# Moving the tensor that takes all loads to a multiple of 4096 bytes in a partition

## The chip, the cores and the metric

The kernel runs on one core of a Trainium2 chip. The metric is the device time of one execution in microseconds (us), the median of several runs.

## The reference

One decoding step: attention of a single query over a long cache of keys and values, a small gated feed-forward block beside it, and a gate that mixes the two.

```python
# x [1,1,512]; k_cache, v_cache [1,32,65536,128]; wq [512,4096]; wo [4096,512]; all bf16
q = (x @ wq) split into 32 heads of 128
scores = einsum("bhqd,bhkd->bhqk", q, k_cache) * 128 ** -0.5
o = einsum("bhqk,bhkd->bhqd", softmax(scores), v_cache)
a = o.reshape(1, 1, 4096) @ wo
b = (silu(x @ w_gate) * (x @ w_up)) @ w_down        # 512 -> 1792 -> 512
g = sigmoid((x * gate_w).sum(-1))
out = g * a + (1 - g) * b
```

The two caches are 537 MB each, and every byte of them is used once.

## The kernel before

A head's keys (16 MiB) come in two loads of 8 MiB, the values likewise. Partition p receives 256 consecutive cache rows of 128 numbers, so a load is 128 partitions with one contiguous stretch of 64 KB each, in HBM and in SBUF alike. This text calls such a stretch a row. Some loads at the beginning and the end have shorter rows: the weights (32 KB, three times 14 KB, 31 KB), the first keys in two halves (32 KB), and the last half of the last head's values in pieces of 128, 64, 32, 16, 12 and 4 cache rows (`tail`), so that little work is left when the last piece has landed.

All of these go into one SBUF tensor, `mem`, 184 KB of a partition (`MEM * KB` numbers of 2 bytes). `at(kb, n)` names n numbers at offset kb in KB. Keys lie at offsets 32 and 0 (`KA`, `KZ`), values at 120 and 96 (`VA`, `VZ`), each 64 KB long, so that the stretches overlap and a load waits for a part of the work on what lay there. All places are whole KB.

The loads are issued by SyncE (SP) in a fixed order: K and V of the heads in turn (`load`, L222 to L249), each behind a wait on how far VectorE (`ktdone`) or TensorE (`pvdone`) has come with the data that it overwrites.

For each head, VectorE transposes the keys out of `mem` into the double buffer `kt` (L322 for the first head, L415 and L422 for the others), 16 operations of 128x2048 words. TensorE multiplies them by the query in `qcur` (L472), the scores stand in one bank, ScalarE turns them into exponentials in `pa` (L288), VectorE moves these between partitions into `pb` (L331), and TensorE multiplies `pb` by the values in `mem` (L525). The value work of a head runs beside the key work of the next.

The tensors lie in a partition in the order in which `sb` allocates them. In the program before, `mem` begins at byte 16512, behind 16 KB that are reserved and four constants of 32 bytes each; `kt` follows at 204928, `qd` at 221312, and the small ones behind it.

Of the kernel before, what the change touches and what calls it, by code (L numbers as in the profile page):

```python
# [5 lines left out]
P = 128  # L6
KB = 512
PR = 32
# [4 lines left out]
BF16 = mybir.dt.bfloat16  # L13
F32 = mybir.dt.float32
U32 = mybir.dt.uint32
# [6 lines left out]
def bass_gated_mix__mha_block_cached__swiglu_ffn__decode_kernel(  # L22
# [27 lines left out]
    MEM = 184  # L50
# [12 lines left out]
    WOJ, WO31 = V0, V0 + 1  # L63

    with ExitStack() as ctx:
        def sb(name, shape, dt):
            return ctx.enter_context(nc.sbuf_tensor(name, shape, dt))

        def psum(name, shape, dt):
            return ctx.enter_context(nc.psum_tensor(name, shape, dt))  # L70
# [10 lines left out]
        psW = psum("psW", [P, 512], F32)  # L81
        psZ = psum("psZ", [P, 512], F32)

        mem = sb("mem", [P, MEM * KB], BF16)
        kt = sb("kt", [P, 2, 2 * PR * 32], U32)
        qd = sb("qd", [P, H, 4, 4], BF16)
        qcur = sb("qcur", [P, 4, 4], BF16)
        pa = sb("pa", [P, 512], BF16)
        pb = sb("pb", [P, 512], BF16)
        orow = sb("orow", [P, 512], F32)  # L90
        ident = sb("ident", [P, 128], F32)
        ones = sb("ones", [P, 2], BF16)
        onesf = sb("onesf", [P, 128], F32)
        hot = sb("hot", [P, 2, 2], F32)
# [536 lines left out]
```

## Time and profile before

| | |
|---|---|
| median of 3 runs | 2518.53 us (2518.48 to 2519.13) |
| span of the profiled execution | 2517.0 us |
| time of the profiled execution beside its span | not listed by itself; the median is 1.5 us above the span |
| instructions | 51694 |
| read from HBM | 1087.77 MB |
| busiest compute engine | PE, 68% of the span |
| granted TensorE clock, mean | 0.721 |

The profile is one execution as the hardware profiler recorded it; the span goes from the first to the last instruction. PE is TensorE's matmuls, PEld its weight loads, DVE is VectorE, ACT ScalarE, SP SyncE. A line such as `L525 PE MATMUL psO<-mem,pb ... x3968 | 1042.3, 429 | 34.5 <-DMA ...` gives a source line, the engine, the operation, what it writes and reads, how often, its busy time in us, the mean of one in ns, and the engine's idle time before it with what ended it. The chain is the work that ended last, followed back from the end; its rows in order of time are start, duration and what it was. In the DMA part, a packet is one row of a load (or the small write that reports a load's completion), and a share is the packets' time as a share of what 16 DMA engines have.

### The profile page before, as it was taken

The page shows a single profiled execution, that of the slowest core. Times are in us where ns is not written, and L with a number is a line of the kernel's source. Part 1 is how long each engine was busy: PE and PEld are TensorE (multiplying, and loading weights), DVE is VectorE, ACT ScalarE, POOL GpSimd, SP SyncE. Part 2 cuts the span into 40 slices and gives each one's busy share as a digit, 9 for nine tenths or more (in the row PEclk, how much of TensorE's full clock was granted, in tenths as well). Part 3 has the DMA queues.
Part 4 walks back from the last instruction along what each step waited for, and adds up shares of the span by engine and source line. Part 5 has one row for each costly group of instructions (what it writes and reads, how often), then busy time and mean ns, then how long its engine had stood idle before and what let it go on. Part 6 is the DMA issues. An engine that isn't in the chain of part 4 may idle for free.

```text
span 2517.0 us, 51694 instructions
## 1 busy us (share of the span) xinstructions
PE 1710.9 (68%) x21624; PEld 979.2 (39%) x21624; DVE 1411.7 (56%) x1683; ACT 64.6 (3%) x195; POOL 0.2 (0%) x4
## 2 busy tenths in 40 slices
PE   4667756667667677676776766766767767667677
PEld 3334433333433334333443333343334433334334
DVE  4764565554655645646456555465564564645653
ACT  0000000000000000000000000000000000000000
POOL 0000000000000000000000000000000000000000
PEclk8577767677677676776776767767767767677677
DMA  9999999999999999999999999999999999999999
GB/s 419 435 433 433 433 433 433 433 434 433 434 433 433 433 433 433 433 433 433 433 433 433 433 433 434 435 433 434 434 433 433 434 434 433 433 433 433 434 433 395
DMA packets 20471, 1087.93 MB, mean 432 GB/s; under 512 B 2283, under 2 KB 2669, under 8 KB 2925
## 3 DMA queue, kind: packets, MB, share of 16 engines
q1 hardware_dynamic: 20452, 1087.78, 99.9%
q8 instruction: 9, 0.15, 0.0%
q14 instruction: 2, 0.01, 0.0%
q10 hardware_dynamic: 8, 0.00, 0.0%
HBM read 1087.77 MB, written 0.00 MB: 432 GB/s over the span
## 4 chain that ended last, share of the span: by engine, by line
DMA 71%; PE 27%; DVE 1%; issue 1%; SPq 0%; ACT 0%; DVEq 0%
DMA mem<-in_A_v_cache_dram 68%; PE psO L525 27%; DMA mem<-in_A_k_cache_dram 2%; DVE kt L322 1%; DMA mem<-in_A_wq_dram 0%; DVE kt L415 0%; SPq L224 0%; PE psM L456 0%; DVE pb L331 0%; PE psS L472 0%; SPq L258 0%; PE psZ L600 0%; DVE sm L336 0%; PE psW L561 0%; PE psM L547 0%
## 5 line engine op out<-in xcount | busy, mean ns | idle before, releaser
L472 PE MATMUL psS<-qcur,kt 128*128 128x4 bf16 x16384 | 573.0, 169 | 728.7 <-DVE kt L415 413.2
L525 PE MATMUL psO<-mem,pb 128*4 128x512 bf16 x3968 | 1042.3, 429 | 34.5 <-DMA mem<-in_A_v_cache_dram 34.1
L472 PEld LDWEIGHTS psS<-qcur,kt 128*128 128x128 bf16 x16384 | 534.0, 105 | 792.1 <-issue 789.7
L422 DVE STREAM_TRANSPOSE kt<-mem 128x2048 uint32<-128x2048 uint32 x248 | 547.6, 2275 | 405.9 <-DMA mem<-in_A_k_cache_dram 405.9
L415 DVE STREAM_TRANSPOSE kt<-mem 128x2048 uint32<-128x2048 uint32 x248 | 551.3, 2280 | 239.3 <-DMA mem<-in_A_k_cache_dram 238.3
L525 PEld LDWEIGHTS psO<-mem,pb 128*4 128x4 bf16 x3968 | 359.8, 93 | 660.4 <-issue 241.3
L331 DVE COPY pb<-pa 32x64 bf16<-32x64 bf16 x1024 | 233.5, 228 | 15.1 <-ACT pa L288 1.5
L338 DVE TENSOR_REDUCE sc<-psM 1x1 f32<-1x128 f32 x32 | 8.9, 279 | 334.9 <-PE psM L547 334.9
L336 DVE TENSOR_REDUCE sm<-psS 128x1 f32<-128x512 f32 x32 | 22.1, 692 | 42.2 <-PE psS L472 42.2
L322 DVE STREAM_TRANSPOSE kt<-mem 128x2048 uint32<-128x2048 uint32 x16 | 35.4, 2277 | 16.9 <-DMA mem<-in_A_k_cache_dram 16.9
L286 ACT ACTIVATE sm<-psM 128x1 f32<-128x1 f32 x32 | 5.5, 171 | 1223.4 <-PE psM L549 1223.4
L282 ACT ACTIVATE oTn<-psT,gcol 128x1 f32 (+1 forms) x31 | 8.2, 264 | 1036.8 <-PE psT L499 1036.8
L499 PE MATMUL psT<-ident,orow 4*128 4x1 f32 x256 | 33.5, 248 | 0.5 <-ACT orow L280 0.5
L499 PEld LDWEIGHTS psT<-ident,orow 4*128 4x128 f32 x256 | 30.8, 186 | 1.2 <-ACT orow L280 0.6
L280 ACT ACTIVATE orow<-psO,sm 4x512 f32<-4x512 f32 x31 | 21.0, 678 | 130.3 <-PE psO L525 126.0
L288 ACT ACTIVATE pa<-psS,sm 128x512 bf16<-128x512 f32 x32 | 22.0, 687 | 1.0
L549 PE MATMUL psM<-sc,onesf 1*128 1x1 f32 x64 | 12.3, 259 | 11.9 <-DVE sc L338 11.9
L561 PE MATMUL psW<-pb,mem 128*128 128x1 bf16 x512 | 14.6, 165 | 6.5 <-DMA mem<-in_A_v_cache_dram 6.0
L549 PEld LDWEIGHTS psM<-sc,onesf 1*128 1x128 f32 x64 | 9.6, 186 | 21.5 <-DVE sc L338 21.5
L561 PEld LDWEIGHTS psW<-pb,mem 128*128 128x128 bf16 x512 | 14.1, 102 | 7.6 <-issue 5.5
L553 PEld LDWEIGHTS psM<-sm,onesf 128*128 128x128 f32 x64 | 9.7, 191 | 14.7 <-issue 13.5
L553 PE MATMUL psM<-sm,onesf 128*128 128x1 f32 x64 | 12.4, 264 | 1.1 <-ACT pa L288 1.1
(72 smaller groups left out, 93.1 us busy)
## 6 DMA issues: line engine op xcount, KB each, us to landing
mem<-in_A_v_cache_dram SPq DMA_DIRECT2D x3, 4096.0 KB, 29.4
mem<-in_A_k_cache_dram SPq DMA_DIRECT2D x2, 4096.0 KB, 38.9
mem<-in_A_wq_dram SPq DMA_DIRECT2D x1, 4096.0 KB, 12.3
mem<-in_A_wo_dram SPq DMA_DIRECT2D x1, 3968.0 KB, 36.6
mem<-in_A_v_cache_dram SPq DMA_DIRECT2D x1, 2048.0 KB, 32.9
mem<-in_B_w_gate_dram SPq DMA_DIRECT2D x1, 1792.0 KB, 16.1
mem<-in_B_w_up_dram SPq DMA_DIRECT2D x1, 1792.0 KB, 21.4
mem<-in_B_w_down_dram SPq DMA_DIRECT2D x1, 1792.0 KB, 25.2
```

Of the source, the lines that this page charges most:

```text
L288: nc.scalar.activation(pa[:], psS[:], ACT.Exp, bias=nbias, scale=SCALE, accum_out=rsum).then_inc(expdone, 1)
L322: nc.vector.transpose(kt[:, i % 2, :].rearrange("p (j r t) -> p r j t", j=2, t=32), src.rearrange("p (r j t) -> p r j t", j=2, t=32)).then ...
L331: last = nc.vector.tensor_copy(dst, sr)
L336: nc.vector.reduce_max(mxs, psS[:], AX_X).then_inc(s_mx, 1)
L415: nc.vector.transpose(kt[:, c % 2, :].rearrange("p (j r t) -> p r j t", j=2, t=32), src.rearrange("p (r j t) -> p r j t", j=2, t=32)).then ...
L422: nc.vector.transpose(kt[:, c % 2, :].rearrange("p (j r t) -> p r j t", j=2, t=32), src.rearrange("p (r j t) -> p r j t", j=2, t=32)).then ...
L472: last = nc.tensor.matmul(psS[:, o:o + 4] if j is None else psS[:, ds(j * (2 * PR) + o, 4)], ktb[b][:, je // 2, r, :, je % 2], qcur[:, je, ...
L499: last = nc.tensor.matmul(psT[:, 0:1], orow[0:4, i * Dh:(i + 1) * Dh], ident[0:4, i:i + 1], start=(i == 0), stop=(i == 3))
L525: last = nc.tensor.matmul(psO[0:4, :], pb[:, k_col[256 * z + r]:k_col[256 * z + r] + 4], vt[:, r * Dh:(r + 4) * Dh], start=(z == 0 and par ...
L549: nc.tensor.matmul(amx, onesf[0:1, :], gm, start=True, stop=True).then_inc(s_ar, 1)
L553: nc.tensor.matmul(Lt, onesf[:], rsum, start=True, stop=True).then_inc(s_L, 1)
L561: last = nc.tensor.matmul(psW[:, 0:1], vt[:, r * Dh:(r + 1) * Dh], pb[:, col:col + 1], start=(r0 + r == 0), stop=(r0 + r == R - 1))
```

## The change

Four small buffers, 3584 bytes together, are allocated ahead of `mem`, and `mem` asks for an alignment of 4096 bytes, which places it at byte 20480; `kt` and the other buffers follow it as before, in nearly the same order. No instruction, wait, load or size changes.

```diff
-        def sb(name, shape, dt):
-            return ctx.enter_context(nc.sbuf_tensor(name, shape, dt))
+        def sb(name, shape, dt, align=32):
+            return ctx.enter_context(nc.sbuf_tensor(name, shape, dt, align_bytes=align))
...
-        mem = sb("mem", [P, MEM * KB], BF16)
-        kt = sb("kt", [P, 2, 2 * PR * 32], U32)
         qd = sb("qd", [P, H, 4, 4], BF16)
-        qcur = sb("qcur", [P, 4, 4], BF16)
         pa = sb("pa", [P, 512], BF16)
         pb = sb("pb", [P, 512], BF16)
+        ident = sb("ident", [P, 128], F32)
+        mem = sb("mem", [P, MEM * KB], BF16, 4096)
+        kt = sb("kt", [P, 2, 2 * PR * 32], U32)
+        qcur = sb("qcur", [P, 4, 4], BF16)
         orow = sb("orow", [P, 512], F32)
-        ident = sb("ident", [P, 128], F32)
```

## The prediction

> **What bounds the kernel now.** I read the page of the profile first: its busy shares, its slices, its DMA part and its chain.
>
> ```profile
> span 2517.0 us, 51694 instructions
> PE 1710.9 (68%) x21624; PEld 979.2 (39%) x21624; DVE 1411.7 (56%) x1683; ACT 64.6 (3%) x195; POOL 0.2 (0%) x4
> DMA  9999999999999999999999999999999999999999
> GB/s 419 435 433 433 433 433 433 433 434 433 434 433 433 433 433 433 433 433 433 433 433 433 433 433 434 435 433 434 434 433 433 434 434 433 433 433 433 434 433 395
> DMA packets 20471, 1087.93 MB, mean 432 GB/s; under 512 B 2283, under 2 KB 2669, under 8 KB 2925
> ...
> q1 hardware_dynamic: 20452, 1087.78, 99.9%
> ...
> DMA 71%; PE 27%; DVE 1%; issue 1%; SPq 0%; ACT 0%; DVEq 0%
> ```
>
> No compute engine is busy for more than 68% of the span. The 16 DMA engines are busy for 99.9% of it on one queue, and the rate is flat at 433 to 435 GB/s in every slice between the first and the last. The kernel is a stream of loads. The chain gives 27% to PE, but the DMA share says that the engines kept moving data meanwhile, so I look at how the chain repeats, in order of time.
>
> ```profile
> 154.46 27.79 DMA mem<-in_A_v_cache_dram
> 182.25 0.04 issue
> 182.29 10.12 PE psO L525 x40
> ...
> 2359.93 28.29 DMA mem<-in_A_v_cache_dram
> ...
> 2477.68 36.14 DMA mem<-in_A_v_cache_dram
> 2513.82 0.05 issue
> 2513.86 0.65 PE psW L561 x16
> 2514.51 0.12 issue
> 2514.63 0.74 PE psZ L600 x7
> 2515.37 0.02 issue
> 2515.39 0.26 ACT fin L300
> ```
>
> One value load is issued at 154.46 us; the same point of the pattern, 19 repetitions later, is 2359.93 us. A repetition holds six loads (three of K, three of V), so a load takes 2205.47 / 114 = 19.346 us of the queue. A load is 8 MiB, 128 rows of 64 KB, eight rows for each of the 16 engines: 19.346 / 8 = 2418.3 ns per row, 433.6 GB/s, which is the rate of the slices. A value load lands 27.8 us after its issue and needs 19.3 us itself, so it lay queued some 8 us behind the load before it. That lead is the cover under which PE's 10.12 us of values and everything else on the compute engines hides. After the last landing at 2513.82 us only 1.8 us of work follows up to 2515.65 us. So what can move the end is the time of a row in the DMA engines, and little else.
>
> **What a row costs.** The DMA view of a window 10 ns long, chosen so that just one packet starts in it, gives that packet's duration: the share times 16 engines times 10 ns. Its bytes are the mean GB/s times 10 ns. Here are loads of 65536, 16384, 4096 and 1024 B rows, a packet of 4 B (a load's completion count), and a 256 B store of the output into HBM (queue 10).
>
> ```profile
> DMA packets 1, 0.07 MB, mean 6554 GB/s; under 512 B 0, under 2 KB 0, under 8 KB 0
> q1 hardware_dynamic: 1, 0.07, 1511.2%
> ...
> DMA packets 1, 0.02 MB, mean 1638 GB/s; under 512 B 0, under 2 KB 0, under 8 KB 0
> q1 hardware_dynamic: 1, 0.02, 381.9%
> ...
> DMA packets 1, 0.00 MB, mean 410 GB/s; under 512 B 0, under 2 KB 0, under 8 KB 1
> q1 hardware_dynamic: 1, 0.00, 99.4%
> ...
> DMA packets 1, 0.00 MB, mean 102 GB/s; under 512 B 0, under 2 KB 1, under 8 KB 1
> q1 hardware_dynamic: 1, 0.00, 28.8%
> ...
> DMA packets 1, 0.00 MB, mean 0 GB/s; under 512 B 1, under 2 KB 1, under 8 KB 1
> q1 hardware_dynamic: 1, 0.00, 5.6%
> ...
> DMA packets 1, 0.00 MB, mean 26 GB/s; under 512 B 1, under 2 KB 1, under 8 KB 1
> q10 hardware_dynamic: 1, 0.00, 9.4%
> ```
>
> That is 2417.9, 611.0, 159.0, 46.1, 9.0 and 15.0 ns. From 4096 to 65536 B the time rises by 2258.9 ns for 61440 B: 27.20 B per ns and engine. Over bytes divided by 27.20, the four loads stand at +8.5, +8.6, +8.4 and +8.4 ns. So a row has a price of its own of about 8.5 ns, whatever its length, and the rest is a straight rate; nothing is paid for each 4 KB or each 256 B inside a row, or the longer rows would show it. The spacing of 2418.3 ns says that rows follow one another without overlap or gap: 2418.3 - 2409.4 = 8.9 ns per row is on the path, completion counts included.
>
> This bounds the change from below. The profile's page has 20471 packets, 2283 of them under 512 B; the other 18188, over 16 engines, make 1136 rows each. If the whole surplus of 8.9 ns went, that would be 1136 x 8.9 ns = 10.1 us. Nothing about an address can give more unless the 27.20 B per ns itself rises, and the rows show one rate from 4 KB to 64 KB.
>
> **The change, part by part.** *The big tensor's address.* In the program before, `mem` begins at byte 16512 of a partition, which is 64 x 256 + 128: every load row begins and ends 128 B past a multiple of 256. Afterwards it begins at 20480, and as all places in `mem` are whole KB, every row begins and ends at a multiple of 256, those of the 8 MiB loads at multiples of 4096 too. No load is added, removed or reordered, and the addresses in HBM stay. All 1136 rows per engine are on the path.
>
> What of the 8.5 ns belongs to the odd start? Below, nothing (the row price is the turnover from one descriptor to the next). Above, all 8.9 ns. The nearest row between is the store: its destination rows in HBM are 256 B apart and start even, and it stands at 15.0 - 256 / 27.20 = +5.6 ns, 2.8 ns less than a load (though its source, `fin`, begins 96 B past a multiple of 256, so it isn't fully even either). The mechanism that I take for likeliest lies between these ends: a row that begins in the middle of a 256 B line is worked from the line's beginning, so the 128 B in front pass through the engine for nothing, 128 / 27.20 = 4.7 ns per row. The end of the row, a half line, costs its bytes alone. That makes 1136 x 4.7 ns = 5.3 us.
>
> [...]
>
> *The small buffers.* `qd`, `pa`, `pb` and `ident` come to lie in front, `kt` and the rest shift. Instructions, waits and queues stay as they are. The reads and writes concerned are these:
>
> ```profile
> L525 PE MATMUL psO<-mem,pb 128*4 128x512 bf16 x3968 | 1042.3, 429 | 34.5 <-DMA mem<-in_A_v_cache_dram 34.1
> L422 DVE STREAM_TRANSPOSE kt<-mem 128x2048 uint32<-128x2048 uint32 x248 | 547.6, 2275 | 405.9 <-DMA mem<-in_A_k_cache_dram 405.9
> L331 DVE COPY pb<-pa 32x64 bf16<-32x64 bf16 x1024 | 233.5, 228 | 15.1 <-ACT pa L288 1.5
> ```
>
> I cost them at nothing. A head takes four loads, 77.4 us, of which DVE works 1411.7 / 32 = 44.1 us and PE 1710.9 / 32 = 53.5 us; DVE idles 405.9 us in front of L422 alone, waiting for K. If an address made DVE a tenth slower, 4 us per head would come out of 33 us of idle time. Without that cover, a tenth on the transposes would be 0.1 x 2 x 547.6 = 110 us (L415 is the same operation for the other half), and a tenth faster as much to the good; with it, neither reaches the end but through the last 1.8 us, under 0.2 us either way. A shorter row brings DVE and PE 0.04 us per load nearer to being late, against 8 us of lead, so nothing new becomes late.
>
> **The sum.** The span is 2517.0 us; the median of the runs is 2518.53, 1.5 us of which lie around the span and stay. 2518.5 - 5.3 = 2513.2 us.
>
> **The rivals.** *The whole surplus goes.* A 64 KB row at an odd start touches 257 lines of 256 B instead of 256. If each touched line costs a full line, 256 / 27.20 = 9.4 ns, that is the whole row price (measured 8.4 to 8.9), and the stream rises to 16 x 27.20 = 435.2 GB/s. For it: a packet of only 4 B takes 9.0 ns, as one line would. Against it: the store with its even destination keeps 5.6 ns. Time: 2518.5 - 10.1 = 2508.4 us (2507.8 with 9.4 ns per row).
>
> *Nothing, or too little.* The 8.5 ns is descriptor turnover, and the address matters not at all, or only by the store's 2.8 ns. Then 2518.5, or 2515.3. For it: the constant is equally compatible with a turnover, and what the engines read lies as it did. This is also the case in which the address is changed as announced and the DMA engines have no use for it.
>
> *Slower.* With source and destination both even, each row's read and write reach their boundaries on the same cycle, where the 128 B offset had kept them apart, and each row stalls once. Taking the same 128 B worth of beats as the price, 4.7 ns per row on the DMA engines is +5.3 us: 2523.8. It decides from 4.4 ns per row on, since 1136 x 4.4 = 5.0 us. The profile shows no stall that an offset could have been avoiding, which speaks against it; it does not show an even row either.
>
> **How the numbers follow.** A measurement of this kernel can tell about 0.2%, 5.04 us, from no change. The 128 B lead-in has a chance of 0.38 (its own range 2512.5 to 2514.5, across the bound of 2513.5: 0.25 beyond it, 0.13 within); the whole surplus 0.32; nothing or too little 0.20; slower 0.10. Faster is 0.25 + 0.32 = 0.57, within 0.2% is 0.13 + 0.20 = 0.33, slower 0.10. The range goes from 2507.8, the whole line, to 2518.9, no change with the runs' spread, and leaves out the slower case.
>
> **What would show it.** In the profile after, the 64 KB packet should take about 2413 ns (2409 for the whole surplus, 2418 for nothing, 2423 for slower), the flat slices should read 434 GB/s (435, 433 and 433 or less in the other cases), and the spacing of value loads six loads apart should fall from 116.08 us by 48 rows x 4.7 ns to 115.85 us. The 1024 B rows of the tail should take 41 ns instead of 46. DVE and PE groups should keep their mean times; if they moved and the end did not, the cover held. I am wrong if the packet keeps its 2418 ns, if its time drops below 2409 ns (the rate itself would then depend on the address), or if the rows shorten and the DMA share falls, which would mean that a wait has taken the bytes' place.

## The result, and the profile after

The changed kernel took 2513.90 us, median of 19 runs (2513.74 to 2514.47), the kernel before 2518.36 us in 19 runs beside it (2518.17 to 2519.13). The ratio is 0.9982, 95% interval 0.9976 to 0.9988: 4.46 us less, 0.18%. The two sets of runs don't overlap.

The page of the profile after, the lines that answer to those of before:

```profile
span 2512.4 us, 51694 instructions
PE 1710.2 (68%) x21624; PEld 979.1 (39%) x21624; DVE 1411.8 (56%) x1683; ACT 64.6 (3%) x195; POOL 0.2 (0%) x4
GB/s 419 435 434 435 434 434 434 434 434 434 436 434 434 434 434 434 434 434 434 434 434 434 434 434 434 434 434 434 434 434 434 434 434 434 434 434 434 434 435 403
...
q1 hardware_dynamic: 20452, 1087.78, 100.0%
...
L525 PE MATMUL psO<-mem,pb 128*4 128x512 bf16 x3968 | 1040.7, 428 | 32.7 <-DMA mem<-in_A_v_cache_dram 32.4
L422 DVE STREAM_TRANSPOSE kt<-mem 128x2048 uint32<-128x2048 uint32 x248 | 547.6, 2275 | 402.3 <-DMA mem<-in_A_k_cache_dram 402.3
L331 DVE COPY pb<-pa 32x64 bf16<-32x64 bf16 x1024 | 233.5, 228 | 15.1 <-ACT pa L288 1.5
```

The engines do the same work in the same time; the DMA queue moves the same packets and bytes. The flat slices read 434 GB/s where they read 433. The chain in order of time shows where the time went. For each kernel, two value loads at like places of the pattern, first before, then after, and for after the last load as well; start, duration from issue to landing:

```profile
154.46 27.79 DMA mem<-in_A_v_cache_dram
...
2437.89 27.75 DMA mem<-in_A_v_cache_dram
```

```profile
154.01 27.64 DMA mem<-in_A_v_cache_dram
...
2433.82 27.49 DMA mem<-in_A_v_cache_dram
...
2473.61 35.63 DMA mem<-in_A_v_cache_dram
```

Counted from landing to landing, 118 loads apart, a load takes (2465.64 - 182.25) / 118 = 19.351 us before and (2461.31 - 181.65) / 118 = 19.319 us after: 31.6 ns per load, or 4.0 ns for each of its eight rows per engine. (The prediction counted from issue to issue, and the second of its two loads took 0.5 us longer to land: 19.346.) The bytes of a load alone are 8 x 2409.4 = 19275 ns, so the surplus per load fell from 75.5 to 43.9 ns. The 1136 rows per engine are 142 loads' worth; 142 x 31.6 ns = 4.5 us. This is the whole gain: the last load lands at 2509.24 us, where it landed at 2513.82, and the span is 4.6 us shorter.

Of the signs that the prediction named, the flat slices read 434 GB/s as forecast, and six loads take 6 x 31.6 ns = 0.19 us less, where 0.23 was forecast. The packet seems to miss. In windows of 10 ns in which one packet starts, a 64 KB row before and one after:

```profile
DMA packets 1, 0.07 MB, mean 6554 GB/s; under 512 B 0, under 2 KB 0, under 8 KB 0
q1 hardware_dynamic: 1, 0.07, 1516.2%
```

```profile
DMA packets 1, 0.07 MB, mean 6554 GB/s; under 512 B 0, under 2 KB 0, under 8 KB 0
q1 hardware_dynamic: 1, 0.07, 1511.2%
```

A row of before can take 2425.9 ns, like this one, as well as the 2417.9 shown in the prediction. After, this row takes 2417.9 ns. One packet does not speak for all of them: each of the two traces has 16000 rows of 64 KB. Before, 99 of 100 are recorded with 2418 to 2428 ns, and the mean is 2421.9; after, 15979 of them have 2418, and the mean is 2418.1. The 386 rows of 1024 B go from 46.9 to 46.0 ns in the mean. So the record of a 64 KB row did shorten, by 3.7 ns, and the 2417.9 that the prediction took for every row was one of the shortest of before. Rows follow one another every 2418.8 ns before and every 2414.9 after, in both cases about 3 ns faster than the mean record: the record of a packet is not the time for which it holds the engine.

### The profile page after: what moved, and what is told of

It is laid out like the page before. It is cut to its first block, busy times and chain, and to the rows that moved or that the text cites. A ratio compares the mean times of both kernels' runs of the same rounds, so it can differ in the third digit from the quotient of the medians.

```text
span 2512.4 us, 51694 instructions
## 1 busy us (share of the span) xinstructions
PE 1710.2 (68%) x21624; PEld 979.1 (39%) x21624; DVE 1411.8 (56%) x1683; ACT 64.6 (3%) x195; POOL 0.2 (0%) x4
## 3 DMA queue, kind: packets, MB, share of 16 engines
q1 hardware_dynamic: 20452, 1087.78, 100.0%
## 4 chain that ended last, share of the span: by engine, by line
DMA 71%; PE 27%; DVE 1%; issue 1%; SPq 0%; ACT 0%; DVEq 0%
DMA mem<-in_A_v_cache_dram 68%; PE psO L525 27%; DMA mem<-in_A_k_cache_dram 2%; DVE kt L322 1%; DMA mem<-in_A_wq_dram 0%; DVE kt L415 0%; SPq L224 0%; PE psM L456 0%; DVE pb L331 0%; PE psS L472 0%; SPq L258 0%; PE psZ L600 0%; DVE sm L336 0%; PE psW L561 0%; PE psM L547 0%
## 5 line engine op out<-in xcount | busy, mean ns | idle before, releaser
L525 PE MATMUL psO<-mem,pb 128*4 128x512 bf16 x3968 | 1040.7, 428 | 32.7 <-DMA mem<-in_A_v_cache_dram 32.4
L422 DVE STREAM_TRANSPOSE kt<-mem 128x2048 uint32<-128x2048 uint32 x248 | 547.6, 2275 | 402.3 <-DMA mem<-in_A_k_cache_dram 402.3
L525 PEld LDWEIGHTS psO<-mem,pb 128*4 128x4 bf16 x3968 | 359.3, 93 | 657.5 <-issue 238.9
```

What stands on the lines that cost most here:

```text
L422: nc.vector.transpose(kt[:, c % 2, :].rearrange("p (j r t) -> p r j t", j=2, t=32), src.rearrange("p (r j t) -> p r j t", j=2, t=32)).then ...
L525: last = nc.tensor.matmul(psO[0:4, :], pb[:, k_col[256 * z + r]:k_col[256 * z + r] + 4], vt[:, r * Dh:(r + 4) * Dh], start=(z == 0 and par ...
```

## The experiments

In what follows, an address is even when it is a multiple of 256 B and odd when it is not, and a line is the 256 B between two such multiples. The theory after the result: a row that starts odd in SBUF costs the engine a fixed piece of time, and the address of `mem` alone decides. The rivals: the small buffers, a unit of 4096 B, a price that grows with the offset (the lead-in of the prediction), a price on the HBM side, and a price per load or per byte instead of per row. All kernels are timed beside the kernel before, which stood at 2518.4 to 2518.5 us.

**The address alone.** Four kernels have the buffers of the change in front and a filler ahead of `mem`, n bytes long:

```diff
-        mem = sb("mem", [P, MEM * KB], BF16, 4096)
+        sb("pad", [P, n // 2], BF16)      # n = 256, 128, 160, 352: mem at 20352, 20224, 20256, 20448
+        mem = sb("mem", [P, MEM * KB], BF16)
```

> The small buffers lie in front as in the change, but the big tensor begins at 20352, 128 B past a multiple of 256, as before. If the address alone made the gain (lead-in and extra-line theories alike): 2518.4 us, the time of before, 64 KB row spacing 2418.3 ns. If the move of the small buffers made it: 2513.9 us, spacing 2414.4 ns.

> The big tensor begins at 20224 = 79 x 256, not a multiple of 512 or 4096. If what counts is a line of 256 B (both the lead-in and the extra-line theory): 2513.9 us. If a multiple of 512 or 4096 is needed: 2518.4 us.

> The big tensor begins 32 B past a multiple of 256. Lead-in theory (the bytes in front of the start pass through): a quarter of the price at 128 B, so 2513.9 + 1.1 = 2515.0 us. Extra-line theory (a row touches 257 lines instead of 256, at a fixed price): 2518.4 us, as for 128 B.

> The big tensor begins 224 B past a multiple of 256. Lead-in theory: 1.75 times the price at 128 B, so 2513.9 + 1.75 x 4.5 = 2521.8 us. Extra-line theory: 2518.4 us. If what counts were the distance to the nearest line, 32 B: 2515.0 us.

Measured: 2518.53, 2513.93, 2519.77 and 2519.75 us. The small buffers have no part in the gain (first run, with the load spacing of before, 19.351 us), and a multiple of 256 is all that is needed (second run); the 4096 of the change is more than that. The third and fourth speak against both theories of the price. At 32 and at 224 B past a line it is the same, 5.8 us, so it doesn't grow with the bytes in front as the lead-in theory asks; and it isn't one price for every odd start either, since 128 B costs 4.6. The chain of the kernel at 20256 has the difference in its load spacing:

```profile
154.39 28.12 DMA mem<-in_A_v_cache_dram
...
2400.24 28.00 DMA mem<-in_A_v_cache_dram
```

(2428.24 - 182.51) / 116 = 19.360 us per load, 9 ns more than at 128 B, 1.1 ns per row.

**The step from 128 to 32.** The same with n = 192, `mem` at 20288:

> The big tensor begins 64 B past a multiple of 256. The runs at 32 and 224 B gave 2519.8 us, the one at 128 B 2518.5 us. If the extra beat of those two comes from a start inside a 128 B unit: 2519.8 us; if from a start inside a 64 B unit: 2518.5 us. The lead-in theory, which asks for 2516.1 us here, is not expected to come back.

Measured: 2518.81 us. That is 0.3 us above the start at 128 B, with the same load spacing of 19.351 us, and 1.0 below those at 32 and 224 B. Of the two units, 64 B fits. The beat of the expectation is its name for the 1.2 us by which the starts at 32 and 224 B stand above the one at 128 B; that the engine works in such pieces no run shows.

**The other side.** The loads inside the loop read from 64 numbers, 128 B, earlier; once with `mem` at 20480, once at 20352:

```diff
-            return cache[0, ds(h, 1)].rearrange("a (b p r) d -> b (a p) (r d)", b=2, p=P)
+            flat = cache.rearrange("a h s d -> (a h s d)")[ds(h * (S * Dh) - 64, S * Dh)]
+            return flat.rearrange("(b p n) -> b p n", b=2, p=P)
```

> The big tensor at 20480 as in the change, but 120 of the 128 loads of keys and values begin 128 B earlier in HBM (they read other cache entries; the bytes and all work are the same). 960 rows per engine. [...] If only the destination counts: 2513.9 us.

> As the run before with the big tensor at 20352: source and destination both 128 B past a multiple of 256 (other cache entries are read). If only the destination counts: 2518.5 us. If each side costs by itself: 2518.5 + 4.5 = 2523.0 us. If what costs is that the two sides are out of step by 128 B: these rows are free again, about 2514.6 us.

Measured: 2513.93 and 2518.40 us. A price of 4.7 ns on each of the 960 rows would have put the first at an estimated 2513.9 + 4.5 = 2518.4 us. A source moved by 128 B costs no time, with an even destination and with an odd one, and being out of step costs none either. Of the two addresses only the one in SBUF counts for the time; whether the read side does more work that hides behind the writes, these runs can't tell.

**Start or end.** `mem` at 20480, and the loop's loads leave out the last 128 B of each row:

```diff
-                sp.dma_start(at(place(kind, h, z), HR * Dh), kv_dram(cache, h)[z])...
+                n = HR * Dh - (0 if isinstance(h, int) else 64)
+                sp.dma_start(at(place(kind, h, z), n), kv_dram(cache, h)[z][:, 0:n])...
```

> The big tensor at 20480; 120 loads leave out the last 128 B of each row (those cache halves-of-entries are not loaded, older bytes are used in their place): the start is even, the end is odd. The bytes alone are 960 x 4.7 ns = 4.5 us less. If an odd start is what costs: 2513.9 - 4.5 = 2509.4 us. If a touched line costs its full 256 B, or an odd end costs as much as an odd start: 2513.2 to 2513.9 us.

Measured: 2510.93 us, between the two forecasts. 4.5 of bytes went and 1.5 us came back: an odd end after an even start costs 1.5 us / 960 = 1.6 ns per row, more than nothing and less than a full line. This excludes that a touched line is charged in full, and the theory that only the start counts was too simple. It also limits what the other runs say. There a row's length is a multiple of 256 B, so a row that starts odd ends odd by the same offset; no run has an odd start with an even end. The 4.6 and 5.8 us are the price of an odd row, start and end together. If the two prices add up, about 1.6 of the 4.6 us / 1136 = 4.1 ns per row belong to the end. A price of the start that grows with the offset, beside one of the end that falls with it at the same rate, would also come out alike at 32 and at 224 B. The end's 1.6 ns at 128 B, where that asks for half of the price, speak against it but do not exclude it.

**Per row or per load.** Loads cut into rows of 16 KB, by reading four pieces from four quarters of the head, so that each piece is a row of its own:

```diff
-            return cache[0, ds(h, 1)].rearrange("a (b p r) d -> b (a p) (r d)", b=2, p=P)
+            hd = cache[0, ds(h, 1)] if not isinstance(h, int) else cache[0, h:h + 1]
+            return hd.rearrange("a (c p b r) d -> b (a p) c (r d)", b=2, p=P, c=4)
...
+                    dst = dst.rearrange("p (c n) -> p c n", c=4)
```

> The big tensor at 20480; 122 loads are cut into rows of 16 KB instead of 64 KB (each row of 64 KB in SBUF takes four pieces from four quarters of the head, the same bytes; only the last head's values, which are loaded as before, are paired with other keys). 122 x 8 x 3 = 2928 more rows per engine. If the rest of 5.0 ns that stands above the bytes after the change is a price per row: 2513.9 + 14.6 = 2528.5 us. If it is a price per load: 2513.9 us.

> The same rows of 16 KB with the big tensor at 20352, 128 B past a multiple of 256. If an odd start is paid per row: 2528.5 + (1136 + 2928) x 3.9 ns = 2544.4 us, 16 us above the even one. If it is paid per load or as a share of the bytes: 4.6 us above the even one.

Measured: 2527.61 and 2546.00 us; the even start cost 0.9 less, the odd one 1.6 more than forecast. The cut was made (queue line of the page, even start: 67300 packets instead of 20452, 2928 more on each engine, for the same bytes):

```profile
q1 hardware_dynamic: 67300, 1087.78, 100.4%
```

So both prices, that of any row and that of an odd one, are paid per row. The chains give them, first for the even and then for the odd start:

```profile
155.16 26.98 DMA mem<-in_A_v_cache_dram
...
2370.35 27.06 DMA mem<-in_A_v_cache_dram
```

```profile
156.01 27.25 DMA mem<-in_A_v_cache_dram
...
2152.80 27.27 DMA mem<-in_A_v_cache_dram
```

Even: (2397.41 - 182.14) / 114 = 19.432 us per load, 113.0 ns more for 24 more rows, 4.71 ns a row. Odd: (2180.07 - 183.26) / 102 = 19.577 us, 225.8 ns more than before, 9.41 ns a row. An odd row at 128 B thus costs 4.70 ns more than an even one. (The cut also changes the order in which HBM is read. The difference of odd and even is free of that; and the records of even rows, 611 ns for 16 KB (14 rows between 1200 and 1200.5 us, 106.9% of 16 engines) and 2418.1 for 64 KB in the mean, stand 8.5 ns (0.3 either way) and 8.7 ns above their bytes, which shows no such effect.) What is left of the surplus for the load itself is 43.9 - 8 x 4.71 = 6.2 ns with even rows and 75.5 - 8 x 9.41 = 0.2 ns with odd ones. That is new: with odd rows the load seems to have no price of its own. With each load come 16 small writes that count its completion, as many as there are engines (the 4 B packets, 9.0 ns each in the mean; between 100 and 2400 us of the kernel after, 119 loads are issued and 1904 packets are under 512 B); does this write hide under the price of odd rows?

**The completion.** The same rows of 16 KB, each cut load issued as four loads of 2 MiB, so that rows stay and completions multiply:

```diff
-                sp.dma_start(dst, kv_dram(cache, h)[z]).then_inc(d[kind + "az"[z]], 16)
+                for c in range(4):
+                    sp.dma_start(dst[:, c, :], src[:, c, :]).then_inc(d[kind + "az"[z]], 16)
...
-                dma = i * 16
+                dma = i * 64
```

> The rows of 16 KB with the big tensor at 20480, but each cut load is issued as four loads of 2 MiB (and the first head's two value loads too): 372 more completion counts per engine, 48 more rows. Load spacing put 4.7 ns on a row and 5.8 ns on a load's completion when the start is even. Theory, the completion is paid: 2527.6 + 0.2 + 372 x 5.8 ns = 2530.0 us. Rival, the 5.8 ns belong to the row or to something else: 2527.8 us.

> The same with the big tensor at 20352, 128 B past a multiple of 256. Load spacing put 9.4 ns on a row and 0.6 ns on a completion. Theory, the completion hides under the price of an odd start: 2546.0 + 0.5 + 372 x 0.6 ns = 2546.7 us. Rival, it is paid as with an even start: 2546.0 + 0.5 + 2.2 = 2548.7 us.

Measured: 2530.23 and 2546.66 us, within 0.3 us of the theory in both, 2.0 us away from the rivals (2.4 for the even start). Load spacing, even, then odd:

```profile
156.47 26.09 DMA mem<-in_A_v_cache_dram
...
2412.64 26.05 DMA mem<-in_A_v_cache_dram
```

```profile
157.70 25.87 DMA mem<-in_A_v_cache_dram
...
2154.89 25.95 DMA mem<-in_A_v_cache_dram
```

(2438.69 - 182.56) / 116 = 19.449 us for four loads, 17.2 ns more for three more completions, 5.7 ns each; with odd rows (2180.84 - 183.57) / 102 = 19.581, 1.5 ns each. (From the medians, less the 48 rows, it is 6.4 and 0.6 ns.) What the runs multiply is loads. That the small write, and not something else that each load brings, takes this time is likely but not shown.

## Why the prediction was right, and where it was not

**What bounds the kernel: right.** Bytes, waits and engine times stayed, the spacing of the loads fell, and the end came earlier by that alone. The cover for the compute engines held: PE and DVE keep their mean times (428 ns in L525 where it was 429, 2275 in L422 as before), and DVE still waits 402.3 us (405.9 before) for keys in front of L422. The kernel at 20352 shows that the small buffers are worth nothing.

**The price of an odd row: the size right by luck, the picture behind it wrong.** 128 / 27.20 = 4.7 ns was forecast for the bytes in front of an odd start, 4.70 ns was measured. But if it were the bytes in front alone, with an end that "costs its bytes alone", 32 B would cost a quarter and 224 B 1.75 times as much. Both cost the same, 5.8 us against the 4.6 of 128 B, and an odd end alone costs 1.6 ns above its bytes. So no run shows that the bytes in front of a start pass through the engine; the 4.7 ns of the sum was the author's estimate for that, and in its place stands the price of an odd row at 128 B, start and end together. What was right is that the SBUF address decides (2513.93 us with the source moved by 128 B) and that the price is paid per row; that 128 B of lead-in have the size of the whole price at this offset is luck. Of the two ends for the price, the store's 2.8 ns was too low and the whole surplus of 8.9 ns too high: 4.71 ns per row stay at an even address. Whether these are a turnover between rows or something else the runs do not show.

**The step that failed: the sum left out the price of a load.** The forecast multiplied 4.7 ns by 1136 rows, 5.3 us, and treated the completions as part of the row. Next to odd rows a load costs 0.2 to 1.5 ns of its own, next to even ones 5.7 to 6.4. The difference, 4.2 to 6.0 ns for each of 142 loads, is 0.6 to 0.85 us. 5.34 less that is 4.5 to 4.7 us; 4.46 was measured. This took the gain from just above the bound of 0.2% that the prediction set for itself to just below it, though with 19 runs each it stands clear of the spread.

**A length read from one packet.** The packet was to shorten to 2413 ns, and the prediction called itself wrong if it kept 2418. A packet of after has 2418, and yet the time fell. The mistake was to take one packet of before, 2417.9 ns, for all. The mean went from 2421.9 to 2418.1 ns, 12.5 and 8.7 ns above the bytes, while the spacing from landing to landing stands 9.4 and 5.5 ns above them. So 8.5 ns was not the mark of an odd row, as nearly every even row has it too; its agreement with the 8.9 ns of the spacing was chance, and that rows follow "without overlap or gap" does not hold for their records, which overlap by some 3 ns. Nor do the lengths show that nothing is paid for each 256 B inside a row: such a price would lie in the 27.20 B per ns.

**The rivals.** The whole surplus would have given 2508.4 us; the rows of 16 KB with an even start show that an even row still costs 4.71 ns. No gain, and a stall of even reads against even writes, are excluded by the result and, for the stall, by the runs with an odd source, which change nothing.

**What stays open.** How the 4.7 ns of an odd row divide between its start and its end, which a run with an odd start and an even end would show; why the starts at 32 and 224 B cost another 1.1 ns per row; and why a load costs 5.7 to 6.4 ns next to even rows and 0.2 to 1.5 next to odd ones. The runs fix the prices, not the circuits.

## What to carry to other kernels

Where the DMA queue is the bound, as here (99.9% of the span), let each row of a load begin and end at a multiple of 256 B in SBUF, and count the gain, for rows that stood 128 B past one, as rows per engine times 4.7 ns, less 4 to 6 ns for each load: 0.18% here with rows of 64 KB, 18.4 us or 0.7% with rows of 16 KB. For the same reason keep rows long, as each costs 4.7 ns even when it is even, and loads few, as each costs 5.7 to 6.4 ns next to even rows. To price a DMA edit, use the spacing of loads from landing to landing, far apart and at like places of the pattern. Do not read it from one packet: rows of before are recorded with 2418 to 2428 ns, more than the gain of 4.0 ns per row.

## What was not expected of the hardware

An even destination makes the packets regular: nearly all 2418 ns after, 2418 to 2428 ns before. Moving the source by 128 B changes nothing in the time (2513.93 us with an even destination, 2518.40 with an odd one). Prices of small things nearly add up: 27.20 B per ns and engine, 4.7 ns per row, another 4.7 ns per odd row at 128 B, 5.7 ns per load next to even rows; with prices like these, from the runs before them, the two last runs were forecast to 0.3 us in 2500.
